# Pauses between the pieces of a norm in a three-stage kernel (attention, mixture of experts, gated layer): other numbers in three tables

## The chip, the cores and the metric

The kernel runs on one core of a Trainium2 chip. The metric is the time of one execution in device microseconds (us). The core's engines are TensorE (PE, matmuls; PEld is its weight load), VectorE (DVE), ScalarE (ACT), GpSimd (POOL) and SyncE (SP, which only issues transfers). Each engine runs its own instructions in the order in which the program wrote them, and waits for others through semaphores.

## The reference, cut to what matters

Attention over 8 heads of 576 positions for 4 batches gives 2304 tokens of 512 numbers. A mixture of 8 experts follows (all tokens through all experts, summed with the weights P). The last layer, in which the change lies, is this:

```python
rms = np.sqrt(np.mean(x * x, axis=-1, keepdims=True) + 1e-06)
xn = x / rms * rms_g
g = xn @ w_gate
silu = g * (1.0 / (1.0 + np.exp(-g)))
val = xn @ w_val
return (silu * val @ w_out).astype(np.float32)
```

Only the division by rms is told of below as "the norm" (rms_g is multiplied into the weights beforehand).

## The kernel before

**Tokens.** The 2304 tokens are three quads of 768 (`qd` 0, 1, 2: the first, second and third quad), each six blocks of 128. All matmuls take float32 operands as a high and a low part, and a product of two 2x2 block matrices is made of seven block products instead of eight. So an operand is kept as seven blocks (k = 0 to 6), each with its high and low part: three plain ones (k = 0 to 2) and four sums and differences (k = 3 to 6).

**Order of the program.** It is written by hand. The main loop counts ticks; whenever `bg.pump()` is called a tick passes, and queues of small steps (`Queue`) hand out those that have come due: an item runs when its lag, counted from the one before it, has passed. Where an item stands in the program is thus set by its lag in ticks; when it runs on the chip, by what its engine finds ahead of it and what it waits for.

**From the experts to the last layer.** The last expert's second half takes the third quad, then the second, then the first. As soon as a quad's sum `acc[:, qd]` is done (DVE, line 1907), four things happen to it:

1. Scaling (`norm_scale`, one run for blocks 0 to 2 and one for 3 to 5): ACT squares three blocks and sums the squares (L1504), DVE makes means (L1507), POOL takes the root (L1511), ACT multiplies three blocks (L1514). `evict_1` puts these steps into `scales[0]` or `scales[1]`.
2. Turning (`turn_tile`, `norm_turn`): PE transposes a block (L1521), ACT copies it back (L1523; in the third quad DVE does every other one, L1525). It first forces out what is left of the block's scaling.
3. Pieces (`norm_blocks`, queue `norm`): blocks i and 3 + i are one piece, so a quad has three. A piece has eight steps: `plain` (ACT L1538 makes high parts, DVE L1539 low parts), `add1` (DVE), `keep` (writes three plain blocks to DRAM, tensor xnd; two transfers, L1551), `add2` (DVE), three times `part` (ACT L1538, DVE L1539), `keep2` (writes the four other blocks; four transfers for the first and second quad, L1579). The first and second quad are written from POOL's queue. All pieces of a quad use the same two scratch areas, for which the accumulators of the next quad serve, so that a `plain` must wait until the `keep` before it has been read out, and a `part` for the `keep2` before it.
4. Loads (`load_block`, L1203, SP's queue): block k of the whole quad, 768 KB with both parts, is read back from xnd into one of nine slots. Plain blocks need the `keep` of all three pieces, the others the `keep2` of all three.

The lags of the pieces come from two tables, one entry per quad (first, second, third): `BLOCK_LAG` is the lag of each step and `BLOCK_GAP` what is added ahead of the second and third piece.

```python
steps = [plain, add1, keep], [add2, lambda: part(0, 1), lambda: part(1, 2), lambda: part(3, 1), keep2]
plain, more = [[(BLOCK_LAG[qd], f) for f in x] for x in steps]
gap = BLOCK_GAP[qd] if i else REST * (qd == 0)
return [(BLOCK_LAG[qd] + gap, steps[0][0])] + plain[1:], more
```

**The last layer** takes the third quad, then the second, then the first, each in two rounds; these six rounds are called 3a, 3b, 2a, 2b, 1a, 1b here (two more passes over all quads follow). A round has 14 steps. In each step PE makes one block product into one of two banks `ub` (L1271, six matmuls), from which ACT copies (L1439) or DVE adds (L1303); a bank is written again two steps later. The order of the blocks in a half round is k = 0, 1, 4, 3, 5, 2, 6. From round 3b on, two down products (L735 to L737, three matmuls each) of the round before stand behind most steps; in 3a transposes of the second quad (steps 3 to 8) and of the first (steps 9 to 14) stand there. "2a.3" below is step 3 of round 2a.

`Queue.add` appends steps whose first lag counts from the queue's last step (a queue idle for long hands out the first at the next tick); `Queue.follow` counts it from now. In the block that the change touches, `n == NGP - 2` is the second quad; the `else` branch serves the third (`NGP - 3`) and the first (`NGP - 1`).

Of the kernel before, what the change touches and what calls it, by code (L numbers as in the profile page):

```python
# [114 lines left out]
def kernel(  # L115
# [51 lines left out]
    LAG = 12  # L167
    FIRST_X = 8
    TURN_AT = (29, 30, 31, 32, 33, 34)
    BLOCK_LAG = (1.4, 1.0, 1.0)  # L170
    BLOCK_GAP = (6, 2, 0)
    LAST_TURN = {2 + i: (2, i) for i in range(6)} | {8 + i: (1, i) for i in range(6)}
    SCALE_LAG = 14
    REST = 10
    Y0_AT = (7, 10, 13, 16, 19)
    READ = 7
    LAST_READ = 16
# [1350 lines left out]
    def norm_blocks(qd, i, spare):  # L1528
# [42 lines left out]
        def part(k, n):  # L1571
            src = (b12, tab, tab, b21)[k]
            parts(src, high_of(k, n), src.bitcast(F32R))
            return 256 * n
# [9 lines left out]
# [6 lines that stand above are left out]
    with tc.manual_schedule():  # L1590
# [117 lines left out]
        for g in range(1, len(groups)):  # L1708
            due = SL * (first[g] // TA) - 4 * (LOOK + (PRE if groups[g][0] else 0)) - DUE
            steps = [step for t in ticks[last[g - 1] + 1 : last[g] + 1] for step in t]  # L1710
# [68 lines left out]
        for idx in range(-LOOK, n1 - LOOK):  # L1779
# [8 lines left out]
            if u.f == 0:  # L1788
                if "x" not in u.cell:
                    fetch(u)  # L1790
                if u.left:
                    bg.add(gate(u.t0, u.n, u.cell["x"]), 20)
                    if u.at:
                        area = fa[:, :1280], fa[:, 1280:3328].bitcast(F32R)
                        steps = sums(0, us[0].cell["x"], *area) if u.at == 1 else []
# [5 lines left out]
                else:  # L1801
# [5 lines left out]
                    steps = []  # L1807
# [20 lines left out]
            if not u.left and u.f == 0:  # L1828
                begin_psum()
                place = db[2], db[5], acc[:, 0, 0], wgc2  # L1830
                steps = []
# [26 lines left out]
        scales = [Queue(bg), Queue(bg)]  # L1858
        turns = {}

        def tile_of(qd, b):
            return 6 * qd + 2 * (b % 3) + b // 3
# [27 lines left out]
        def evict_1(n, k):  # L1890
            g, hh, qd = groups[n]
            half, col = OUT[k]
            a = acc[:, qd, 3 * half : 3 * half + 3]
            ps = threes[PAIR[k]].rearrange("p (m n) -> p m n", m=3)
            if col is None:
                a = a.rearrange("p m (c n) -> p m c n", c=2)
                ps = ps[:, :, None, :].to_broadcast([P, 3, 2, 256])
            else:
                a = a[:, :, 256 * col : 256 * (col + 1)]
            if (hh == 0 or g < E - 1) and k in (0, 2, 3, 4):  # L1900
                bg.drain(("expert", qd, half, col if half else None))
                nc.scalar.copy(a, ps)  # L1902
            elif (g, hh) == (E - 1, 1):
                if k in (0, 2, 3):
                    bg.drain(("expert", qd, half, col if half else None))
                for m in range(3):
                    nc.vector.scalar_tensor_tensor(
                        out=a[:, m], in0=ps[:, m], scalar=prob[:, tile_of(qd, 3 * half + m), g : g + 1],
                        in1=a[:, m], op0=ALU.mult, op1=ALU.add,
                    )  # L1910
                    bg.vector(512 if col is None else 256)
            else:
                nc.vector.tensor_tensor(out=a, in0=ps, in1=a, op=ALU.add)  # L1913
                bg.vector(1536 if col is None else 768)
            at = 2 * (g - E_STD) + hh + 1
            if n % NQD == NQD - 1:
                if n < NGP - 1:
                    product_2[at](k)
                elif k >= 3:
                    prepare_2(E, (0, 2, 1, 3)[k - 3], LAST_READ if k == 3 else STEP)  # L1920
            if (hh == 0 or g < E - 1) and k in (1, 5, 6):
                args = (g, hh, qd) + ((1, 0) if k == 1 else (0, None) if k == 5 else (1, 1))
                if early is None:
                    close_region(*args)
                else:
                    early.append(args)
            if (g, hh) == (E - 1, 1) and k >= 5:
                steps = norm_scale(qd, 3 * (k - 5))
                if n == NGP - 2:
                    scales[k - 5].follow([(SCALE_LAG, lambda: None)] + steps, ("scale", qd))  # L1930
                else:
                    short = 0.5 if n == NGP - 1 else 1
                    scales[k - 5].add([(short * lag, f) for lag, f in steps], ("scale", qd))

        early = []

# [105 lines left out]
        for n, (g, hh, qd) in enumerate(groups):  # L2042
# [12 lines left out]
            if n == 2:  # L2055
                waiting_for, early = early, None
                bg.add([lambda a=a: close_region(*a) for a in waiting_for], 12, bg.now + 8)
            if n in Y0_AT:
                i = 4 * Y0_AT.index(n)
                first_sums([divmod(x, 6) for x in range(i, min(i + 4, NTILE))])  # L2060
# [19 lines left out]
            for r in range(2):  # L2080
# [7 lines left out]
                for i, (wk, xk, which, begins) in enumerate(PROD):  # L2088
                    product((a, b)[which], w_block(region(g, j), wk), x_view(xmap[xk]), begins)
                    outcome_1(i, a, b, rd)  # L2090
                    if n < 2 and i in ((3, 6) if (n, r) == (0, 0) else (1, 6)):
# [4 lines left out]
                        steps = [lambda to=free_part: columns_2(totals, to)]  # L2096
# [100 lines left out]
        steps = 14  # L2197
        done = None
        nmap, nfree = xmap, free
        for n, (p, qd) in enumerate(passes):  # L2200
# [10 lines left out]
            for j in range(NG // 2):  # L2211
# [10 lines left out]
                if fresh and p:  # L2222
                    k = PROD[0][1]
                    load_block(nmap[k], True, qd2, k)
                for ci, s in enumerate((2 * j, 2 * j + 1)):
# [5 lines left out]
                    if fresh and p == 0 and ci == 1:  # L2231
                        k = PROD[0][1]
                        left.append((nmap[k], True, qd2, k))
                    for i, (wk, xk, which, begins) in enumerate(PROD):
# [23 lines left out]
                        if fresh and ci == 1 and i < 6:  # L2258
                            k = PROD[i + 1][1]
# [52 lines left out]
```

## Time and profile before

| | us |
|---|---|
| three runs | 2055.06, 2059.94, 2064.48 (median 2059.94) |
| profiled execution | 2053.64, of which its span (first to last instruction) is 2051.9 |
| PE busy | 2001.2 (98% of the span) |
| DVE, ACT, POOL busy | 1585.4, 1315.9, 296.4 |

The first two lines are times of whole executions; the profile's rows count from the first instruction of the profiled one. PE's matmuls are pipelined, so "busy" also holds stretches at a lower clock. The mean granted clock of PE is 0.991 of full speed.

### The profile page before, as it was taken

What the parts mean: (1) busy time and instruction counts of PE and PEld (TensorE: products, weight loads), DVE (VectorE), ACT (ScalarE), POOL (GpSimd) and SP (SyncE); (2) the same over time, 40 slices, a digit from 0 to 9 for tenths busy, and PEclk for the clock granted to TensorE, in tenths of its full rate; (3) what the DMA queues carried; (4) which work ended last, traced back from release to release, by engine and by line L of the source; (5) the groups of instructions that cost most, each with busy time, mean ns of one, the idle gap of its engine ahead of it and who ended that gap; (6) DMA issues with size and microseconds to landing.
All of it is one profiled execution on the core that took longest, in us unless ns stands there. A gap on an engine that the chain in (4) does not pass through costs nothing.

```text
span 2051.9 us, 37537 instructions
## 1 busy us (share of the span) xinstructions
PE 2001.2 (98%) x13611; PEld 1921.3 (94%) x13611; DVE 1585.4 (77%) x3364; ACT 1315.9 (64%) x2938; POOL 296.4 (14%) x340
## 2 busy tenths in 40 slices
PE   8999999999999999999999999999998988999999
PEld 7889888999999999999999999999998877888998
DVE  3677757889887888878787798888888657988645
ACT  6766335777777778878787777767766633423422
POOL 6443300001111111111011111111100220000000
PEclk9999999999999999999999999999999999999999
DMA  7688586577989889898888879778777775454341
GB/s 193 166 240 215 172 277 208 199 247 181 293 221 264 238 223 263 219 288 213 241 213 229 253 184 264 190 211 236 201 216 221 251 232 198 120 187 157 127 151 62
DMA packets 343577, 434.24 MB, mean 212 GB/s; under 512 B 81248, under 2 KB 242976, under 8 KB 343264
## 3 DMA queue, kind: packets, MB, share of 16 engines
q1 hardware_dynamic: 301360, 352.47, 52.8%
q0 software_dynamic: 42032, 79.38, 20.8%
q8 instruction: 107, 1.75, 0.3%
q14 instruction: 78, 0.64, 0.1%
HBM read 301.75 MB, written 130.02 MB: 210 GB/s over the span
## 4 chain that ended last, share of the span: by engine, by line
PE 83%; DVE 7%; DMA 4%; ACT 3%; issue 2%; POOL 1%; SPq 0%; POOLq 0%; DVEq 0%; ACTq 0%
PE ub L1271 36%; PE db L1881 28%; PE db L737 2%; PE db L736 2%; PE db L735 2%; DMA xt<-xdt 2%; PE psh L735 2%; PE psh L736 2%; PE psh L737 2%; PE psy L735 1%; PE ps_s L505 1%; PE psy L736 1%; PE psy L737 1%; PE ps_o L574 1%; DVE fa L1303 1%
## 5 line engine op out<-in xcount | busy, mean ns | idle before, releaser
L1271 PE MATMUL ub<-xt,w1t 128*128 128x384 f32 x2328 | 470.9, 339 | 12.2 <-DMA xt<-xnd 6.5
L1271 PEld LDWEIGHTS ub<-xt,w1t 128*128 128x128 f32 x2328 | 397.1, 190 | 18.2 <-issue 7.8
L1271 PE MATMUL ub<-xx,w1t 128*128 128x384 f32 x1956 | 394.5, 338 | 10.8 <-DMA xx<-xnd 7.6
L1881 PE MATMUL db<-w2t,ht 128*128 128x256 f32 x2772 | 380.9, 282 | 3.4 <-DVE ht L1299 1.9
L1881 PEld LDWEIGHTS db<-w2t,ht 128*128 128x128 f32 x2772 | 368.7, 189 | 3.9 <-DVE ht L1299 2.1
L1271 PEld LDWEIGHTS ub<-xx,w1t 128*128 128x128 f32 x1956 | 332.5, 190 | 17.0 <-issue 6.9
L1881 PE MATMUL db<-w2t,hx 128*128 128x256 f32 x2520 | 345.9, 282 | 2.2 <-DVE hx L1299 1.7
L1881 PEld LDWEIGHTS db<-w2t,hx 128*128 128x128 f32 x2520 | 333.9, 189 | 3.2 <-DVE hx L1299 1.9
L1303 DVE TENSOR_TENSOR fa<-ub,fa 128x384 f32<-128x384 f32 x360 | 199.2, 554 | 166.3 <-PE ub L1271 158.9
L1422 ACT ACTIVATE fa<-fa 128x384 f32<-128x384 f32 x252 | 132.4, 525 | 168.5 <-DVE fa L1303 168.1
L1950 POOL DMA_DIRECT2D y1d<-acc x99 | 113.9, 1150 | 798.3 <-DVE acc L1913 323.3
L1299 DVE TENSOR_TENSOR ht<-fa,ht 128x384 fp32r<-128x384 f32 x344 | 189.0, 551 | 22.2 <-ACT ht L1296 21.3
L1943 ACT ACTIVATE acc<-acc,prob 128x256 f32<-128x256 f32 (+1 forms) x351 | 190.7, 572 | 12.5 <-DVE acc L1913 12.2
L1296 ACT ACTIVATE ht<-fa 128x384 fp32r<-128x384 f32 x344 | 177.5, 518 | 27.4 <-DVE fa L1474 25.8
L1299 DVE TENSOR_TENSOR hx<-fa,hx 128x384 fp32r<-128x384 f32 x316 | 174.1, 551 | 26.1 <-ACT hx L1296 24.8
L1296 ACT ACTIVATE hx<-fa 128x384 fp32r<-128x384 f32 x316 | 162.4, 519 | 44.3 <-DVE fa L1474 40.9
L1377 DVE TENSOR_TENSOR fa<-fa 128x384 f32<-128x384 f32 x336 | 185.3, 551 | 5.2
L1414 ACT COPY fa<-ub 128x384 f32<-128x384 f32 x252 | 119.4, 474 | 93.1 <-PE ub L1271 92.3
L1913 DVE TENSOR_TENSOR acc<-db,acc 128x768 f32<-128x768 f32 (+1 forms) x117 | 142.9, 1221 | 39.0 <-PE db L1881 38.8
L1902 ACT COPY acc<-db 128x768 f32<-128x768 f32 x156 | 124.6, 799 | 14.5 <-PE db L1881 9.4
L1439 ACT COPY fa<-ub 128x384 f32<-128x384 f32 x108 | 51.6, 479 | 104.3 <-PE ub L1271 102.2
L1031 DVE TENSOR_TENSOR w1t<-fa,w1t 128x256 fp32r<-128x256 f32 (+1 forms) x160 | 83.4, 524 | 19.1 <-ACT w1t L1028 19.1
(269 smaller groups left out, 3091.9 us busy)
## 6 DMA issues: line engine op xcount, KB each, us to landing
xt<-xdt SPq DMA_DIRECT2D x111, 768.0 KB
xx<-xdt SPq DMA_DIRECT2D x92, 768.0 KB
y1d<-acc POOLq DMA_DIRECT2D x72, 384.0 KB, 8.4
y1d<-acc POOLq DMA_DIRECT2D x36, 768.0 KB, 8.6
xt<-xnd SPq DMA_DIRECT2D x25, 768.0 KB
xx<-xnd SPq DMA_DIRECT2D x24, 768.0 KB
fa<-in_moe_w_dram SPq DMA_DIRECT2D x56, 256.0 KB
raw<-in_moe_w_dram SPq DMA_DIRECT2D x52, 256.0 KB
```

The costliest lines, as they stand in the source:

```text
L1271: nc.tensor.matmul(ps[:, :TH], w[i][:, c], x[:, k, c], start=first and c == 0 and n == 0, stop=c == 1 and n == 2, skip_group_check=True,)
L1296: nc.scalar.activation(h[0], src, func)
L1299: engine.tensor_tensor(out=h[1], in0=src, in1=h[0].bitcast(F32), op=ALU.subtract)
L1303: nc.vector.tensor_tensor(out=out, in0=ps, in1=more, op=ALU.add)
L1377: nc.vector.tensor_tensor(**kw)
L1414: nc.scalar.copy(z[nm], ps)
L1422: nc.scalar.activation(z[nm], z[nm], AF.Relu)
L1881: nc.tensor.matmul(spot(k, m), hm[x], w[y], start=BEGIN[k] and r == 0 and m != 1 and i == 0, stop=r == 1 and i == 2, skip_group_check=True,)
L1902: nc.scalar.copy(a, ps)
L1913: nc.vector.tensor_tensor(out=a, in0=ps, in1=a, op=ALU.add)
L1943: nc.scalar.activation(a, a, AF.Copy, scale=prob[:, tile_of(qd, b), g : g + 1])
L1950: nc.gpsimd.dma_start(out=y, in_=t, accum_op=ALU.add)
```

## The change

Four numbers change, and one is new. The second quad's steps have a lag of 0.8 ticks instead of 1.0, and nothing is added ahead of its second and third piece (2 before). The first quad gets 2 added ticks instead of 6 there. The scaling of the third and of the first quad begins with an empty step of 3 ticks counted from now (`follow`) instead of at once (`add`); within it the first quad keeps its half lags. No instruction is added or taken away; PE's and POOL's instructions stand in the same order as before.

```diff
-    BLOCK_LAG = (1.4, 1.0, 1.0)
-    BLOCK_GAP = (6, 2, 0)
+    BLOCK_LAG = (1.4, 0.8, 1.0)
+    BLOCK_GAP = (2, 0, 0)
...
     SCALE_LAG = 14
     REST = 10
+    AFTER = 3
...
                 else:
                     short = 0.5 if n == NGP - 1 else 1
-                    scales[k - 5].add([(short * lag, f) for lag, f in steps], ("scale", qd))
+                    scales[k - 5].follow([(AFTER, lambda: None)] + [(short * lag, f) for lag, f in steps], ("scale", qd))
```

The new line moves all later lines by one: what is L1504 before is L1505 in the changed kernel.

On ACT, at the beginning of round 3a, these rows stand between the last expert and the layer's first copies. L1514 with `acc` is the multiplication of the scaling, L1504 the square; the first six multiplications belong to the second quad, all other scaling here to the first. L1439 is the copy that empties bank `ub`, L1523 the copy of a turned block. Before:

```order
L1514 ACTIVATE acc<-acc,cv 128x512 x5
L1504 ACTIVATE cv<-acc 128x512 x2
L1514 ACTIVATE acc<-acc,cv 128x512
L1504 ACTIVATE cv<-acc 128x512
L1514 ACTIVATE acc<-acc,cv 128x512 x3
L1504 ACTIVATE cv<-acc 128x512 x2
L1439 COPY fa<-ub_4251 128x384
L1504 ACTIVATE cv<-acc 128x512
L1457 ACTIVATE fa<-fa 128x384
```

In the changed kernel the same place reads:

```order
L1515 ACTIVATE acc<-acc,cv 128x512 x6
L1505 ACTIVATE cv<-acc 128x512 x3
L1440 COPY fa<-ub_4251 128x384
L1458 ACTIVATE fa<-fa 128x384
L1440 COPY fa<-ub_4251 128x384
L1515 ACTIVATE acc<-acc,cv 128x512 x2
L1505 ACTIVATE cv<-acc 128x512
```

Three multiplications and two squares of the first quad moved from ahead of the round's first L1439 to behind it; a third square, which stood right behind it, moved further back too.

On ACT in round 3b, L1538 makes the high parts of the second quad's pieces, L1457 is the sigmoid and L1439 the copy out of `ub`. Before, these rows stand there, from the second piece's `plain` (the first two L1538) to the first row of the third piece's `plain` (the last row, behind the copy of step 3b.8):

```order
L1538 ACTIVATE acc<-acc 128x512
L1538 ACTIVATE acc<-acc 128x256
L1439 COPY fa<-ub_4251 128x384
L1439 COPY fa<-ub_4252 128x384
L1538 ACTIVATE acc<-acc 128x256
L1457 ACTIVATE fa<-fa 128x384
L1538 ACTIVATE acc<-acc 128x512
L1457 ACTIVATE fa<-fa 128x384
L1538 ACTIVATE acc<-acc 128x256
L1457 ACTIVATE fa<-ub_4251 128x384
L1439 COPY fa<-ub_4252 128x384
L1538 ACTIVATE acc<-acc 128x512
```

In the changed kernel, from the second piece's three `part` steps (the first three rows):

```order
L1539 ACTIVATE acc<-acc 128x256
L1539 ACTIVATE acc<-acc 128x512
L1539 ACTIVATE acc<-acc 128x256
L1440 COPY fa<-ub_4251 128x384
L1440 COPY fa<-ub_4252 128x384
L1539 ACTIVATE acc<-acc 128x512
L1539 ACTIVATE acc<-acc 128x256
L1458 ACTIVATE fa<-fa 128x384
L1539 ACTIVATE acc<-acc 128x256
L1458 ACTIVATE fa<-fa 128x384
L1539 ACTIVATE acc<-cv 128x512
```

The two L1439 in the middle are those of steps 3b.3 and 3b.4 in both. Before, the second piece's parts stand behind them, spread between three sigmoids; in the changed kernel the parts stand ahead of them and the third piece's `plain` right behind.

On SP, ahead of round 1a, L1203 loads the first quad's seven blocks; L840 and L882 fetch and store other weights. Before:

```order
L840 DMA cv<-in_moe_w_out_dram 128x512
L882 DMA m2o<-cv 128x256
L1203 DMA xx<-xnd 128x2x768 x2
L840 DMA fa<-in_moe_w_out_dram 128x512
L882 DMA m2o<-cv 128x256
L1203 DMA xt<-xnd 128x2x768 x4
L1203 DMA xx<-xnd 128x2x768
```

In the changed kernel:

```order
L1204 DMA xx<-xnd 128x2x768
L841 DMA cv<-in_moe_w_out_dram 128x512
L883 DMA m2o<-cv 128x256
L1204 DMA xx<-xnd 128x2x768
L1204 DMA xt<-xnd 128x2x768 x2
L841 DMA fa<-in_moe_w_out_dram 128x512
L1204 DMA xt<-xnd 128x2x768
L883 DMA m2o<-cv 128x256
L1204 DMA xt<-xnd 128x2x768
```

The first load moved ahead of a fetch and a store, and the third to fifth ahead of the second store; the last two (one more xt, and an xx behind the last row) still stand behind it.

## Rows read from the trace of the kernel before

**Rows 1.** Page: busy us and share of the span by engine.
```profile
PE 2001.2 (98%) x13611; PEld 1921.3 (94%) x13611; DVE 1585.4 (77%) x3364; ACT 1315.9 (64%) x2938; POOL 296.4 (14%) x340
```

**Rows 2.** Waits of PE from 1500 to 1800: total, times, longest us.
```profile
PE ub L1271 <- DMA xx<-xnd: 7.6, 2, 6.5
PE ub L1271 <- DMA xt<-xnd: 5.8, 1, 5.8
```

**Rows 3.** Timeline of PE: start, us, what; in brackets idle before it.
```profile
1539.70 0.60 PE L1521 MATMUL db<-ident,acc 128*128 128x128 f32 x4
...
1592.70 2.25 PE L1271 MATMUL ub<-xt,w1t 128*128 128x384 f32 x12
1599.13 2.24 PE L1271 MATMUL ub<-xt,w1t 128*128 128x384 f32 x6 [4.18 <-ACT fa L1439]
...
1618.54 0.59 PE L1271 MATMUL ub<-xt,last_r 128*128 128x384 f32 x2
...
1649.65 2.26 PE L1271 MATMUL ub<-xx,w1t 128*128 128x384 f32 x6 [6.46 <-DMA xx<-xnd]
...
1699.38 1.29 PE L1271 MATMUL ub<-xx,w1t 128*128 128x384 f32 x6 [1.15 <-DMA xx<-xnd]
1701.38 2.05 PE L1271 MATMUL ub<-xx,w1t 128*128 128x384 f32 x6 [0.71 <-DVE cv L854]
...
1711.43 4.10 PE L1271 MATMUL ub<-xt,w1t 128*128 128x384 f32 x12 [5.83 <-DMA xt<-xnd]
```

**Rows 4.** Stretches: length, busy us (count) by engine, PE's granted clock, DMA.
```profile
1540.00:1560.00 20.00, 18.28 (x133) 17.88 (x132) 16.68 (x38) 11.48 (x24) 0.00 (x0) 1.00 0.50 143
1572.00:1580.00 8.00, 5.84 (x36) 5.64 (x36) 7.50 (x18) 4.96 (x12) 0.00 (x0) 0.79 0.85 237
1599.10:1603.40 4.30, 4.27 (x17) 4.14 (x18) 1.28 (x3) 2.70 (x6) 0.85 (x1) 0.60 1.06 407
1600.00:1616.00 16.00, 16.00 (x101) 15.62 (x100) 9.78 (x19) 13.34 (x29) 2.61 (x3) 0.92 0.84 315
1649.60:1653.60 4.00, 3.95 (x12) 3.83 (x13) 0.00 (x0) 0.48 (x1) 0.00 (x0) 0.50 1.01 398
1701.40:1705.60 4.20, 4.20 (x12) 3.39 (x12) 3.29 (x9) 0.74 (x2) 0.00 (x0) 0.59 1.03 395
1711.40:1715.40 4.00, 3.97 (x13) 3.83 (x14) 0.00 (x0) 0.48 (x1) 0.00 (x0) 0.52 1.03 411
```

**Rows 5.** Chain that ended last: start, us, what.
```profile
1635.93 5.12 DMA xnd<-acc
...
1641.16 8.35 DMA xx<-xnd
```

**Rows 6.** The same chain 60 us later.
```profile
1699.33 7.66 DMA xnd<-acc
...
1707.00 4.29 DMA xt<-xnd
```

**Rows 7.** Timeline of POOL: second quad, second `keep2` and third `keep`.
```profile
1632.01 3.07 POOL L1579 DMA_DIRECT2D xnd<-acc  x4 [5.74 <-ACT acc L1538]
1635.07 1.69 POOL L1551 DMA_DIRECT2D xnd<-acc  x2
```

**Rows 8.** Timeline of ACT.
```profile
1540.92 0.53 ACT L1422 ACTIVATE fa<-fa 128x384 f32<-128x384 f32 x1 [1.15 <-DVE fa L1303]
...
1591.53 0.63 ACT L1504 ACTIVATE cv<-acc 128x512 f32<-128x512 f32 x1 [1.05 <-DVE acc L1907]
...
1595.40 1.94 ACT L1514 ACTIVATE acc<-acc,cv 128x512 f32<-128x512 f32 x3 [1.16 <-POOL cv L1511]
1598.62 0.46 ACT L1439 COPY fa<-ub 128x384 f32<-128x384 f32 x1
...
1625.53 0.48 ACT L1439 COPY fa<-ub 128x384 f32<-128x384 f32 x1 [0.56 <-PE ub L1271]
...
1632.85 0.94 ACT L1538 ACTIVATE acc<-acc 128x512 fp32r<-128x512 f32 x2
```

## The prediction

> **What bounds the kernel now.** I began with the page: PE is busy 98% of the span [rows 1], so only stretches in which PE stops can give much. Four numbers for the norm can move only the passage from the experts to the last layer, so I looked at PE's waits there, then at the timeline around each. PE waits twice for blocks in `xx` and once for one in `xt`, 7.6 and 5.8 us, all read back from xnd [rows 2]. The reader is to see three stops:
>
> - Stop A, 3a.3: PE waits 4.18 us for ACT's copy of the bank that 3a.1 filled [rows 3].
> - Stop B, 2a.1: 6.46 us for a load [rows 3]. The chain of waits goes back from that load (8.35 us) to the third `keep` (its write took 5.12 us) [rows 5]. POOL issued this `keep` right behind the second piece's `keep2`, with no pause between the two [rows 7].
> - Stop C, 1a.1 to 1a.3: 1.15, 0.71 and 5.83 us, 7.7 in all [rows 3]. The last comes from a write of `keep2` (7.66 us) and the load behind it (4.29 us) [rows 6].
>
> Each stop costs more than its length, since the granted clock is down afterwards: 0.50 behind B, 0.59 and 0.52 around C, 0.60 behind A [rows 4], between full speed and half, as stretches mix 2.4 and 1.2 GHz. Busy time times (1 - clock) is what that costs: 3.95 x 0.50 = 2.0 us at B, 4.20 x 0.41 + 3.97 x 0.48 = 3.6 at C, 4.27 x 0.40 = 1.7 at A. So A costs 5.9, B 8.5 and C 11.3 us. No more than these 25.7 us can be had.
>
> **Part 1: the first quad's scaling, later (stop A).** Before, ACT reached the copy for A at 1598.62, though PE had filled the bank by about 1594 (twelve matmuls of two products from 1592.70, 2.25 us) [rows 3, 8]. Ahead of the copy stood the first quad's scaling, among it three multiplications that had waited 1.16 us for POOL's root and took 1.94 us [rows 8]. In the changed order only three squares stand there. The first begins when it did, at 1591.53, and its sums wait for DVE as before [rows 8]; at 0.63 us and a short read-out each, three end at about 1593.7. The copy then takes 0.46 and is done by 1594.5, before PE ends its second product at 1594.95. Stop A goes: +5.9 us.
>
> The work isn't gone; it now stands inside 3a. In 16 us of that round ACT was busy 13.34 us [rows 4], so 2.7 us were free. Into it go three multiplications (1.94), two squares (0.63 and a read-out, some 0.7 each) and, since the pieces come earlier, some 1.3 us of high parts (a `plain`, 0.94, and one `part` of under half of that) [rows 8]: 4.6 us, 2 more than fit. PE can be only two steps ahead of the copies. Following ACT's changed order row by row, I find PE short of a copied bank by 0.5 us near 3a.7, 0.3 at 3a.9 and 2.0 at 3a.10, where five rows of the norm stand ahead of the copy: -2.8 us. Is the clock lost there too? Waits of 1.15 and 0.71 us within 2 us were followed by a clock of 0.59 [rows 3, 4], so I count 1.7 us for these as well. Part 1 gives 5.9 - 2.8 - 1.7 = +1.4 us. Bounds: 0 (all of it comes back as waits for ACT) and 5.9.
>
> **Part 2: the third quad's scaling, later.** `follow` starts it three ticks later, but the turning forces out what is left, so its first block is multiplied just ahead of the transposes. In the changed ACT order the three multiplications stand behind the L1422 that ran at 1540.92, which had waited 1.15 us for DVE; the first transposes ran at 1539.70 [rows 3, 8]. With ACT and DVE a little freer before, I get the first block at 1541.2, a wait of 1.5 us. Half of it is made good, since PE waits for DVE's copy after the next two groups anyway: -0.7 us. Bounds: 0 and -2.3 (L1422 where it was, one multiplication of 0.65 behind it, nothing made good). The waits of under a microsecond between 1540 and 1560 left the clock at 1.00 [rows 4], so no clock is counted here.
>
> **Part 3: the second quad's pieces (stop B).** The third piece's `plain` ran at 1632.85; in the new order it stands right behind the copy of 3b.4, which ran at 1625.53 [rows 8]: 6.9 us earlier against PE. With PE itself ahead by 1.4 (part 1) that is about 1624.5. Now what was slack becomes a wait: this `plain` writes where the second piece's `keep` is still being read out. By the changed order that `keep` is issued near 1619.5, and read out some 5 us later, by the 5.12 of the row [rows 5], so `plain` runs near 1625. The third `keep` then queues on POOL behind the second `keep2` (3.07 us): issued near 1626.5 instead of 1635.07 [rows 7], written 5.9 us later (5.12 from its second transfer on) at 1632.4. Its load, taken at 8.35 us again [rows 5] because writes are still under way, ends near 1640.8. PE came to 2a.1 at 1643.2 (1649.65 - 6.46) [rows 3], and comes at 1641.8 with part 1. The load is in time by 1 us.
>
> Two things come late in its place. DVE makes the low parts of that `plain` only when the `keep` before it is read out, and the sums of 3b.5 and 3b.6 (L1303) stand behind it: PE waits about 1.0 us at 3b.7 and 0.6 at 3b.8. And the third `keep2` is written at about 1640, after which the four sum blocks follow each other at the pace of the queue (4.29 us for one alone [rows 6], near 2 each in a row); 2a.4 and 2a.6 may wait 0.7 us. Part 3 gives 8.5 - 1.6 - 0.7 = +6.2. Bounds: 8.5, and 2 (as much as part 1 brings PE forward, the pieces held wholly by the reuse of their areas).
>
> **Part 4: the first quad's pieces (stop C).** Its pieces begin some six steps earlier, as they follow the second quad's, and the last `keep2` stands at 2b.4 instead of 2b.13: nine steps of (1643.2 - 1618.54) / 14 = 1.76 us [rows 3], 15.9 us. Stop C is 7.7 us of waiting. The loads then go out when the blocks of 2b free their slots. On SP the third to fifth come ahead of a store that they stood behind; the last two remain behind it, and they are needed only at 1a.6 and 1a.7. So C goes in full: +11.3. Bounds: 6, if the clock is lost to other waits in the same place or the last loads come late, and 11.3. What hides the norm in 2a and 2b is DVE and ACT with free time, but a denser norm may hold a copy: -0.7 (0 to -2).
>
> **The sum.** 1.4 - 0.7 + 6.2 + 11.3 - 0.7 = 17.5 us. The profiled execution took 2053.64 (its span 2051.9 and 1.7 around it), so it becomes 2036.1. It is 6.3 below the median of the three runs; taken from the median of 2059.94 the sum gives 2042.4, which I round to 2042 as what runs of the changed kernel should show. The bounds add to 5.7 us (0 - 2.3 + 2 + 6; the last -2 is part of C's 6) and 25.7 us.
>
> **Rivals.** Changes under 0.5% (10.3 us) can't be told from none here.
>
> (a) *Short waits that keep the clock down.* Each of the new waits (3b.7 and 3b.8 together, 2a.4, 2b) is followed by half-speed matmuls. For: 0.79 granted from 1572 to 1580, when PE was busy 5.84 of 8 us [rows 4]. Against: the clock of 1.00 from 1540 to 1560. At 1.7 us for each of two to three, 5 us go: 2047. The Trainium skill, "TensorE: Matmul & The Clock Gate", section on HAM oscillation, says that waits for transfers between groups of matmuls throttle PE again, so that each group starts cold; by that rule the number of waits counts and this case holds. The trace bears it out only for waits of near 2 us and more, as the two stretches show.
>
> (b) *The pieces stand earlier but don't run earlier.* Each `part` waits for the `keep2` before it to be read out, so a quad's three pieces keep a period of their own: the last two `keep2` writes issued 7 us apart already, POOL hardly idle between them [rows 7]. Then B keeps most of its 8.5, the first quad follows late, and C loses its lower bound's 5 us. 1.4 - 0.7 + 2 + 6 - 0.7 = 8 us: 2052, not to be told from no change. Against it: the second piece's `keep2` had waited 5.74 us for ACT [rows 7], which is pause, not period.
>
> (c) *Slower.* In 3b ACT and DVE wait for writes inside their queues, PE stops at every few steps, and the clock stays at its lower level. A product of six matmuls took 2.26 us at B, as long as two at full speed (2.25) [rows 3], so at worst a round of 24.7 us takes twice as long. One round takes the whole gain; a round and a half costs 37 us: 2079. It decides when waits of 2 us come as often as from 1572 to 1580 (2.2 us idle in 8 [rows 4]), all through 3b and half of 2a. Against it: in 3a, where ACT is fuller than in 3b, the clock was 0.92 even with stop A's end in it [rows 4].
>
> **How the numbers follow.** The forecast as worked out, all three stops nearly gone, 0.52 (2035 to 2046); (a) 0.22 at 2047; (b) 0.17 at 2052; (c) 0.05; the rest, 0.04, is more than forecast (A's full 5.9 kept). The range of 2031 to 2054 leaves out (c), the end of (b) and the runs that lie lower than 25.7 us of gain. Faster by over 0.5% (below 2049.6): the forecast, most of (a), the rest: 0.78. Within 0.5%: (b) and a little of (a): 0.17. Slower: 0.05.
>
> **What would show it.** Right: no wait of PE for a load from xnd above 1.5 us at 2a.1 and 1a.1 to 1a.3; granted clock near 1.00 after them; the wait for L1439 at 3a.3 gone, and one of about 2 us for L1440 near 3a.10 in its place; POOL's third `keep` of the second quad some 8 us earlier; a wait of 1 to 1.5 us ahead of the first transposes of the third quad. Wrong: 2a.1 still waits more than 3 us, with ACT or DVE waiting for a write ahead of a piece (then b), or a clock under 0.8 over all of 3b without one long wait (then c). The forecast is most open in part 1: if ACT's backlog in 3a is absorbed, 4.5 us more come.

## The result, and the profile after

| | before | changed | ratio, 95% interval |
|---|---|---|---|
| median, first comparison | 2057.53 us (4 runs) | 2041.12 us (4 runs) | 0.9916 [0.9889, 0.9943] |
| median, second comparison (E5 below) | 2055.32 us (11 runs) | 2041.21 us (6 runs) | 0.9931 [0.9913, 0.9949] |
| profiled execution | 2053.64 us | 2041.57 us | |
| its span, mean clock of PE | 2051.9 us, 0.991 | 2039.6 us, 0.995 | |

The change made the kernel faster by 0.7 to 0.8%, near the forecast of 2042. By medians it gained 16.4 and 14.1 us, with intervals of 12 to 23 and of 10 to 18. From one profiled execution to the other it gained 12.1 us, where the sum said 17.5. So some terms are wrong, and the trace says which.

PE's busy time hardly moved. From the page of the changed kernel (answers to [rows 1]):

```profile
PE 1998.0 (98%) x13611; PEld 1918.3 (94%) x13611; DVE 1586.4 (78%) x3364; ACT 1316.0 (65%) x2938; POOL 296.9 (15%) x340
```

PE's waits from 1500 to 1800 in the changed kernel (answers to [rows 2]; total, times, longest):

```profile
PE db L1522 <- ACT acc L1524: 2.0, 1, 2.0
PE db L738 <- DVE ht L1300: 2.0, 1, 2.0
...
PE ub L1272 <- DMA xt<-xnd: 0.8, 1, 0.8
PE ub L1272 <- DMA xx<-xnd: 0.8, 2, 0.5
```

The loads from xnd, 13.4 us of waiting before, now cost 1.6. New are waits for ACT and DVE, the two of 2.0 us above all. Where do they stand? PE runs the same instructions in the same order in every kernel here, so the start of one row in both traces gives PE's lead over the kernel before at that place, and the change of the lead between two places says what the stretch between them gave. First six marks in the trace of before, beside 1592.70 and 1618.54 of [rows 3] (timeline of PE):

```profile
1538.64 1.23 PE L1881 MATMUL db<-w2t,hx 128*128 128x256 f32 x9
...
1603.35 0.60 PE L1521 MATMUL db<-ident,acc 128*128 128x128 f32 x4
...
1640.24 0.51 PE L1271 MATMUL ub<-xx,w2t 128*128 128x384 f32 x2
...
1653.97 0.40 PE L736 MATMUL db<-w2t,hx 128*128 128x512 f32 x1
...
1697.37 0.39 PE L735 MATMUL db<-w2t,ht 128*128 128x512 f32 x1
...
1716.76 2.25 PE L1271 MATMUL ub<-xt,w1t 128*128 128x384 f32 x12
```

The same eight rows in the changed kernel, with the waits between them (timeline of PE; answers to [rows 3]):

```profile
1539.76 1.23 PE L1882 MATMUL db<-w2t,hx 128*128 128x256 f32 x9
1542.21 0.66 PE L1522 MATMUL db<-ident,acc 128*128 128x128 f32 x4 [1.22 <-ACT acc L1515]
...
1594.42 3.29 PE L1272 MATMUL ub<-xt,w1t 128*128 128x384 f32 x18
...
1599.06 0.60 PE L1522 MATMUL db<-ident,acc 128*128 128x128 f32 x4
...
1605.83 0.65 PE L1522 MATMUL db<-ident,acc 128*128 128x128 f32 x4 [2.01 <-ACT acc L1524]
...
1608.61 1.31 PE L1272 MATMUL ub<-xt,w1t 128*128 128x384 f32 x6 [0.65 <-DVE fa L1461]
...
1611.43 1.33 PE L1272 MATMUL ub<-xt,w1t 128*128 128x384 f32 x6 [1.07 <-ACT fa L1440]
...
1618.92 0.59 PE L1272 MATMUL ub<-xt,last_r 128*128 128x384 f32 x2
...
1623.71 0.50 PE L738 MATMUL db<-w2t,ht 128*128 128x512 f32 x1 [2.00 <-DVE ht L1300]
...
1637.70 2.38 PE L1272 MATMUL ub<-xt,w2t 128*128 128x384 f32 x12 [1.04 <-DVE fa L1461]
...
1644.78 0.51 PE L1272 MATMUL ub<-xx,w2t 128*128 128x384 f32 x2
...
1647.56 1.24 PE L1272 MATMUL ub<-xx,w1t 128*128 128x384 f32 x6
...
1650.70 0.40 PE L737 MATMUL db<-w2t,hx 128*128 128x512 f32 x1
...
1697.97 0.39 PE L736 MATMUL db<-w2t,ht 128*128 128x512 f32 x1
...
1698.67 2.26 PE L1272 MATMUL ub<-xx,w1t 128*128 128x384 f32 x12
...
1705.64 2.25 PE L1272 MATMUL ub<-xt,w1t 128*128 128x384 f32 x12
```

The lead is 1538.64 - 1539.76 = -1.12 us before the norm even begins (it arose in the stages ahead, so it isn't of the change), and 1716.76 - 1705.64 = +11.12 at the end. The stops A (3a.3), B (2a.1, at 1647.56) and C (1a.1 to 1a.3, from 1698.67) have no wait left. Their gain is partly given back between them.

The table holds this balance for all runs: what PE's lead over the kernel before gained (+) or lost (-) between the marks, in us. The columns end at the rows that stand at 1592.70 (3a.1), 1603.35, 1618.54 (3b.1), 1640.24, 1653.97, 1697.37 and 1716.76 before. The first column holds part 2 (0.45 us) and a jitter of -1.1 to +0.8 that comes and goes.

| run | to 3a.1 | stop A | rest of 3a | 3b | stop B | 2a, 2b | stop C | sum |
|---|---|---|---|---|---|---|---|---|
| forecast | -0.7 | +5.9 | -4.5 | -1.6 | +8.5 | -1.4 | +11.3 | +17.5 |
| changed | -0.60 | +6.01 | -4.67 | -4.16 | +7.81 | -3.87 | +11.72 | +12.24 |
| E1 scaling only | +0.30 | +6.01 | -5.44 | -0.20 | +0.82 | -0.58 | -0.38 | +0.53 |
| E2 tables only | -0.23 | +0.01 | -0.17 | -2.62 | +7.80 | -4.42 | +11.72 | +12.09 |
| E3 second quad only | -0.30 | 0.00 | -0.17 | -4.15 | +7.79 | -3.48 | +10.93 | +10.62 |
| E4 first quad only | +0.75 | -0.63 | -0.49 | -0.01 | +1.53 | -4.02 | +11.64 | +8.77 |
| E5 changed, again | +0.32 | +6.01 | -6.04 | -4.13 | +7.78 | -3.91 | +11.73 | +11.76 |
| E6 DVE turns | -1.57 | +6.01 | -4.30 | -2.58 | +7.56 | -4.85 | +11.73 | +12.00 |
| E7 lag 0.7 | +0.33 | +6.01 | -6.06 | -3.48 | +8.54 | -4.61 | +11.73 | +12.46 |
| E8 scaling spread | -0.71 | +6.01 | -5.63 | -4.15 | +7.80 | -3.84 | +11.73 | +11.21 |
| E9 weights later | +0.32 | +6.04 | -2.65 | -4.38 | +7.80 | -4.38 | +11.73 | +14.48 |
| E10 first quad rests | -0.60 | +6.01 | -4.83 | -4.15 | +8.62 | -3.94 | +11.73 | +12.84 |
| E11 lag 0.7, weights | -0.60 | +6.03 | -2.65 | -3.33 | +8.54 | -4.42 | +11.72 | +15.29 |
| E12 combined | +0.75 | +6.01 | -2.62 | -3.71 | +7.28 | -4.25 | +11.73 | +15.19 |

The two executions of the changed kernel (changed, E5) agree within 0.1 us in most columns, but differ by 0.9 ahead of 3a.1 and by 1.4 in the rest of 3a. The runs of one kernel scatter by several microseconds. So the medians say whether a kernel is faster, and the balance says where.

### The profile page after: what moved, and what is told of

The parts are those of the page before. It is cut to its first block, busy times and chain, and to the rows that moved or that the text cites. A ratio compares the mean times of both kernels' runs of the same rounds, so it can differ in the third digit from the quotient of the medians.

```text
span 2039.6 us, 37535 instructions
## 1 busy us (share of the span) xinstructions
PE 1998.0 (98%) x13611; PEld 1918.3 (94%) x13611; DVE 1586.4 (78%) x3364; ACT 1316.0 (65%) x2938; POOL 296.9 (15%) x340
## 4 chain that ended last, share of the span: by engine, by line
PE 84%; DVE 6%; DMA 4%; ACT 2%; issue 2%; POOL 0%; SPq 0%; DVEq 0%; POOLq 0%; ACTq 0%
PE ub L1272 37%; PE db L1882 28%; PE db L738 2%; PE db L737 2%; PE db L736 2%; DMA xt<-xdt 2%; PE psh L736 2%; PE psh L737 2%; PE psh L738 2%; PE psy L736 1%; PE ps_s L506 1%; PE psy L737 1%; PE psy L738 1%; PE ps_o L575 1%; DVE fa L1304 1%
## 5 line engine op out<-in xcount | busy, mean ns | idle before, releaser
L1304 DVE TENSOR_TENSOR fa<-ub,fa 128x384 f32<-128x384 f32 x360 | 199.7, 555 | 158.2 <-PE ub L1272 152.0
L1300 DVE TENSOR_TENSOR ht<-fa,ht 128x384 fp32r<-128x384 f32 x344 | 189.4, 552 | 20.7 <-ACT ht L1297 19.7
L1300 DVE TENSOR_TENSOR hx<-fa,hx 128x384 fp32r<-128x384 f32 x316 | 174.5, 552 | 27.9 <-ACT hx L1297 26.9
```

The source lines that it names most:

```text
L1300: engine.tensor_tensor(out=h[1], in0=src, in1=h[0].bitcast(F32), op=ALU.subtract)
L1304: nc.vector.tensor_tensor(out=out, in0=ps, in1=more, op=ALU.add)
```

## The experiments

Each has runs of the kernel before on the same chip beside it.

**E1 to E4: which edit does what.** E1 has the tables of before, E2 the scaling of before, E3 and E4 one quad's part of the tables.

```diff
# E1: the scaling of the change, the tables of before
+    AFTER = 3
...
-                    scales[k - 5].add([(short * lag, f) for lag, f in steps], ("scale", qd))
+                    scales[k - 5].follow([(AFTER, lambda: None)] + [(short * lag, f) for lag, f in steps], ("scale", qd))
# E2: the tables of the change (E3: GAP 6, 0, 0), the scaling of before
-    BLOCK_LAG = (1.4, 1.0, 1.0)
-    BLOCK_GAP = (6, 2, 0)
+    BLOCK_LAG = (1.4, 0.8, 1.0)
+    BLOCK_GAP = (2, 0, 0)
# E4: LAG and scaling of before
-    BLOCK_GAP = (6, 2, 0)
+    BLOCK_GAP = (2, 2, 0)
```

> The scaling of the third and first quad begins three ticks later, as in the changed kernel; the tables of the pieces are those of before. Theory S (the waits of 3a come from the scaling): stop A goes, 6.0 us; the three waits of the second half of 3a that the changed kernel showed (2.01, 0.65 and 1.07 us for ACT and DVE) stand here too and take 4.5 back; the first transposes wait 1.2 us, 0.5 after what is made good. Round 3b begins 1.0 us earlier, stops B and C stay, and B's load follows PE only in part: 0 to 1.5 us faster than before, 2053 against a median of 2054 to 2058. Theory P (those waits come from the pieces that stand earlier): no wait above 0.5 us in the second half of 3a, 5.5 us kept up to 3b.1; with B and C growing only in part, 2.5 to 5.5 us faster.

> The tables of the pieces as in the changed kernel; the scaling begins at once, as before. Stop A stays: 4.2 us and the clock behind it. Theory S: no waits in the second half of 3a, but those of 3b (2.00 for DVE at the first down products with a clock of 0.62 behind it, 1.04 at 3b.8) stay, as they come from the second piece's plain and sums ahead of the DVE row that PE needs; B and C gone. Sum: -4.3 in 3b, +7.8 at B, -3.9 in 2a, +12.0 at C, so 11.6 us faster than before, the same as the changed kernel within 1.5 us, ratio 0.9944. Theory P: the waits of 3a come too, 3.7 to 4.5 us less: 7 us faster, ratio 0.9965.

> Only the second quad's two numbers (lag 0.8, nothing added); first quad's pause of 6 ticks and the scaling as before. The last keep2 of the first quad then stands at 2b.8, between 2b.13 of before and 2b.4 of the changed kernel. Theory R (either half of the table is enough for stop C, since its loads can go out only from 2b.7 on when slots come free): the write and the load of 12 us (7.66 + 4.29) from 2b.8 end seven steps later at about 1a.1, so C shrinks from 7.7 us of waiting to 0 to 3: B +7.8, 3b -4.3, 2a -2 to -4, C +8 to +12: 10 to 13 us faster. Theory H (each half of the table gives its share of C): C keeps 4 us of waiting and its clock, 4 to 7 us faster.

> Only the first quad's pause, 2 ticks instead of 6; the second quad's pieces and the scaling as before. Its last keep2 stands at 2b.9. Stops A and B stay, round 3b has no new wait. Theory R (either half of the table is enough for C): keep2 is written and loaded by about 1a.2, one step ahead of the first sum block, C keeps 0 to 3 us of waiting and loses little clock: 8 to 12 us faster than before. Theory H: C keeps half, 4 to 6 us faster. If the waits of 2a (0.78, 0.54, 0.52 and 1.05 us, 3.9 us in all in the changed kernel) come from the first quad's denser pieces they show here as well, 1 to 3 us.

| | median us | ratio to before, 95% interval |
|---|---|---|
| E1 | 2055.64 | 0.9997 [0.9987, 1.0007] |
| E2 | 2042.65 | 0.9944 [0.9929, 0.9958] |
| E3 | 2042.86 | 0.9937 [0.9923, 0.9952] |
| E4 | 2046.03 | 0.9955 [0.9941, 0.9969] |

The later scaling alone is worth nothing that the runs can tell, and the tables alone can't be told from the whole change (12.09 us by the balance, 12.24 and 11.76 with the scaling). E1 shows theory S: stop A goes (+6.01), and the rest of 3a takes 5.44 back, without any earlier piece; E2, which keeps stop A, has no loss there. Theory P falls. E1's timeline of PE shows the new wait in 3a:

```profile
1607.45 0.66 PE L1522 MATMUL db<-ident,acc 128*128 128x128 f32 x4 [3.04 <-ACT acc L1524]
```

E3 and E4 show theory R: either half of the table takes stop C away (+10.93 and +11.64 of 11.72). The two halves aren't independent: 10.62 + 8.77 = 19.4 against E2's 12.09. Each of them alone still leaves one of the first quad's loads late: PE waits 0.98 and 1.01 us for it at 1a.6, and 1.9 and 1.7 us are lost from 1716.76 to 1800 (0.1 in E2). The loss in 3b comes with the second quad's numbers alone (E4: -0.01), the one in 2a and 2b with either.

**E5 to E8: what holds 3a and 3b.** E5 is the changed kernel once more. E6 lets DVE copy the second quad's turned blocks, E7 lowers the lag once more, E8 spreads the scaling.

```diff
# E6, in norm_turn
-        if qd < NQD - 1 or t % 2:
+        if qd == 0 or qd == 2 and t % 2:
# E7
-    BLOCK_LAG = (1.4, 0.8, 1.0)
+    BLOCK_LAG = (1.4, 0.7, 1.0)
# E8
-                    short = 0.5 if n == NGP - 1 else 1
+                    short = 1 if n == NGP - 1 else 1
```

> The changed kernel once more, as a yardstick for the next ones on the same chip. By the first four runs the tables of the pieces bring all of the gain and the scaling none: a ratio of 0.992 to 0.9945 to the kernel before, the same as the tables alone (0.9944) within what the intervals tell apart. If the scaling did bring its predicted 1.4 us or more beside the tables, it lies at 0.9925 or below.

> The changed kernel, and in 3a the six turned blocks of the second quad are copied back by DVE instead of ACT. Theory S (ACT's total work is the limit in the second half of 3a: 4.00 of 4 us busy in three windows): six copies of 0.57 us, about 3 us, leave ACT, and DVE, busy 1.1 to 1.8 of 4 us up to 1608, has room; the waits of 2.01, 0.65 and 1.07 us shrink to 1 us or less, and the lost 4.65 us of 3a to 1: 3 to 4.5 us faster than the changed kernel. Theory O (the order on the queues is the limit, since DVE's mean waits for ACT's squares and everything behind it on DVE waits too): the same waits appear with DVE's copies as their cause, and the time is that of the changed kernel within 1 us.

> The changed kernel with a lag of 0.7 instead of 0.8 for the second quad: its second piece's plain stands at 3a.13 instead of 3a.14, the third at 3b.2 instead of 3b.4. Theory B (the pieces have reached the period that the reuse of their areas sets): the third keep is issued no more than 1 us earlier against PE, DVE rows wait longer behind pieces, the loss in 3b grows from 4.15 us to 5 to 7: 1 to 3 us slower than the changed kernel. Theory W (the wait of 2.00 us at the first down products of 3b comes only from where the second piece's plain and sums stand): they now stand ahead of the rows of 3b.1, the wait goes and with it the clock of 0.62 behind it: 2 to 3.5 us faster.

> The changed kernel with the first quad's scaling at whole lags instead of half ones, so that it is spread over 3a.1 to 3a.12 instead of 3a.1 to 3a.8. Theory S1 (the scaling makes a heap on ACT in the middle of 3a): fewer rows stand ahead of the copies of 3a.7 to 3a.10, the three waits fall from 3.73 us to 1 or 2: 2 to 3 us faster than the changed kernel. Theory S2 (it is ACT's total that counts, and what is spread meets the pieces and the first quad's turning at 3a.9 to 3a.14): the waits move back to the second half of the round in the same sum, and transposes wait for a block not yet scaled: the same time within 1 us.

| | median us | ratio to before, 95% interval |
|---|---|---|
| E5 | 2041.21 | 0.9931 [0.9913, 0.9949] |
| E6 | 2039.92 | 0.9920 [0.9903, 0.9937] |
| E7 | 2040.41 | 0.9925 [0.9907, 0.9943] |
| E8 | 2040.89 | 0.9928 [0.9908, 0.9949] |

None can be told from E5. E5 can't be told from E2 (0.9944) either, so no gain of the scaling beside the tables is shown. E6 takes work off ACT and E8 spreads it, and 3a loses as before them (-4.30 and -5.63): ACT's work alone isn't the limit there. What else is, stands in ACT's timeline. Before, the high part of the weights `w2t` (L1138, L1139 in the others) began without a wait; in the changed kernel and in E5 ACT stood still ahead of it (a fence each, in this order):

```profile
1603.92 0.64 ACT L1138 ACTIVATE w2t<-w2t 128x512 fp32r<-128x512 f32 x1
```

```profile
1602.69 0.63 ACT L1139 ACTIVATE w2t<-w2t 128x512 fp32r<-128x512 f32 x1 [1.74 <-DMA w2t<-m2o]
```

```profile
1601.52 0.63 ACT L1139 ACTIVATE w2t<-w2t 128x512 fp32r<-128x512 f32 x1 [3.09 <-DMA w2t<-m2o]
```

The chain that ended last, in the changed kernel (start, us, what), goes through this transfer, and so does PE's wait of 2.01 us for L1524 at 1605.83:

```profile
1590.38 12.29 DMA w2t<-m2o
1602.69 0.63 ACT w2t L1139
...
1605.30 0.47 ACT acc L1524
```

SP issued the transfer behind the loads from xnd, and the queue was full: between 1585 and 1605 the DMA view of the changed kernel lists these, with the size of each, and the engines' share was 103%:

```profile
q1 hardware_dynamic: 3168, 7.73, 103.2%
...
xt<-xnd SPq DMA_DIRECT2D x3, 768.0 KB
xx<-xnd SPq DMA_DIRECT2D x3, 768.0 KB
...
w2t<-m2o SPq DMA_DIRECT2D x4, 256.0 KB
```

That the full queue makes it slow is likely, but no run emptied the queue. It was as full before (103.1%). In the seven traces in which ACT waits for this transfer, ACT could begin 12.2 to 12.4 us after its issue. Before, it was issued at 1588.28, so by an estimate from these it landed at about 1600.6, and ACT, held up by the scaling ahead of stop A, came at 1603.92. Stop A had been the cover of these weights.

The balance says how much of 3a's loss this is. Where ACT waits for `w2t`, 1.74 to 3.09 us, the loss less this wait is 2.35 to 3.09 us (changed 2.93, E5 2.95, E1 2.65, E6 2.35, E7 3.09, E8 2.68, E10 2.94). In E5 ACT waits 1.35 us longer than in the changed kernel, and 3a loses 1.37 more. So the wait passes to PE nearly in full, and a part of about 2.6 us remains that isn't the transfer.

In E6 the stall only changes its name: DVE's low part (L1142) waits for ACT's high part, then DVE's mean (L1508) 1.29 us for ACT's squares, and PE for the DVE row behind both (E6, timeline of ACT, of DVE and of PE):

```profile
1604.18 0.63 ACT L1139 ACTIVATE w2t<-w2t 128x512 fp32r<-128x512 f32 x1 [1.95 <-DMA w2t<-m2o]
```

```profile
1604.84 0.69 DVE L1142 TENSOR_TENSOR w2t<-w2t 128x512 fp32r<-128x512 f32 x1 [1.70 <-ACT w2t L1139]
...
1607.50 0.55 DVE L1304 TENSOR_TENSOR fa<-ub,fa 128x384 f32<-128x384 f32 x1
```

```profile
1608.11 1.32 PE L1272 MATMUL ub<-xt,w1t 128*128 128x384 f32 x6 [2.21 <-DVE fa L1304]
```

So theory O was right about E6's time and about DVE's wait for the squares, though the first cause is the transfer, which neither theory had named.

E7 answers for the pieces. POOL's third `keep` of the second quad, in the changed kernel, in E5 and in E7 (timeline of POOL, a fence each; the last row of [rows 7] is that of before):

```profile
1630.19 1.69 POOL L1552 DMA_DIRECT2D xnd<-acc  x2 [0.93 <-ACT acc L1539]
```

```profile
1629.04 1.68 POOL L1552 DMA_DIRECT2D xnd<-acc  x2 [0.94 <-ACT acc L1539]
```

```profile
1627.53 1.69 POOL L1552 DMA_DIRECT2D xnd<-acc  x2
```

Against 3b.1 (1618.92, 1617.77 and 1616.25) it is issued 11.27, 11.27 and 11.28 us later; before it was 1635.07 - 1618.54 = 16.53. The change brought it 5.3 us forward; the next step of the lag brings nothing. This is theory B's mark. In the changed kernel neither ACT nor DVE waits for a write to xnd between 1600 and 1650; in E7 ACT does, ahead of the third piece's first `part` (timeline of ACT):

```profile
1628.58 0.42 ACT L1539 ACTIVATE acc<-acc 128x256 fp32r<-128x256 f32 x1 [2.84 <-DMA xnd<-acc]
```

Theory B's price isn't paid: the wait of 2.00 at 3b.2 shrinks to 0.57, waits of 0.92 (3b.2), 1.36 (3b.7) and 0.54 (3b.8) come for it, and 3b loses 3.48 instead of 4.13.

**E9 to E12: the weights' high parts later, the first quad later, both and more.**

```diff
# E9, E11, E12: the wait ahead of the last layer's first high part
-    LAST_READ = 16
+    LAST_READ = 20
# E10 (E12: 13)
-    REST = 10
+    REST = 16
# E11, E12
+    BLOCK_LAG = (1.4, 0.7, 1.0)
# E12 also: the third quad's scaling by add
```

> The changed kernel; the four high parts of the last layer's weights w2t that ACT makes in 3a are due four ticks later (20 instead of 16), nothing else. Theory D (with stop A gone ACT reaches the first of them before its transfer has landed, and waits 1.74 to 3.09 us for it with the copies of 3a behind it, as every run with the later scaling showed): the wait for w2t goes, PE's wait for L1524 with it, the loss in 3a falls from 4.65 to 5.9 us to 1 to 2, and 3 to 4.5 us more of stop A are kept: 2 to 4.5 us faster than the changed kernel. Theory S (ACT's total work in the second half of 3a): ACT's work is the same, the waits of 3a only take other places, same time within 1 us.

> The changed kernel; the first quad's first piece starts six ticks later (a rest of 16 instead of 10), at 2a.2 instead of 3b.12, its last keep2 stands at 2b.7 instead of 2b.4. Theory T (round 2a loses 3.9 us because the first quad's first writes and pieces fall between the second quad's loads): PE's waits for xt and xx in 2a (0.73, 0.64 and 0.50 us) go or halve and those for DVE move: 1 to 3 us faster than the changed kernel, if stop C stays gone. Theory K (those loads wait for the second quad's own last keep2 and then follow each other at the pace of the queue): the loads land as before, the waits stay, and with keep2 at 2b.7 stop C takes 0 to 2.7 us back (2b.8 gave 2.7): same, or up to 3 us slower.

> The changed kernel with both edits: lag 0.7 for the second quad and the weights' high parts four ticks later. If the two gains are independent (3b kept about 1.2 us more with 0.7, the weights 2 to 4.5 us): 3 to 6 us faster than the changed kernel, a ratio to the kernel before of 0.990 to 0.992. If PE's earlier arrival only waits again (at 2a.1 to 2a.6 for the second quad's loads, which start by the writes and not by PE): half of it, 1 to 3 us.

> The changed kernel with four edits: lag 0.7 for the second quad, the weights' high parts four ticks later, the third quad's scaling at once again, and a rest of 13 for the first quad. By the pieces measured so far: 1.2 us in 3b, 2 to 3 us in 3a, 0.5 us at the third quad's first transposes, 0 to 1.5 us in 2a: 4 to 6 us faster than the changed kernel, a ratio to the kernel before of 0.989 to 0.991, if they add. If PE, coming earlier, waits for the second quad's loads in 2a instead, a ratio of 0.991 to 0.992, as the two edits alone gave (0.9915). The wait at the first transposes shows part 2 by itself: 1.22 us with the later scaling, gone here.

| | median us | ratio to before, 95% interval |
|---|---|---|
| E9 | 2038.12 | 0.9912 [0.9898, 0.9926] |
| E10 | 2041.18 | 0.9926 [0.9911, 0.9941] |
| E11 | 2038.69 | 0.9915 [0.9902, 0.9928] |
| E12 | 2040.80 | 0.9931 [0.9915, 0.9948] |

E9 settles 3a. ACT doesn't wait for `w2t` any more, PE's wait for L1524 is gone, and 2.65 us are lost instead of 4.67 and 6.04 (timeline of ACT, then of PE):

```profile
1607.67 0.67 ACT L1139 ACTIVATE w2t<-w2t 128x512 fp32r<-128x512 f32 x1
```

```profile
1605.55 1.31 PE L1272 MATMUL ub<-xt,w1t 128*128 128x384 f32 x6 [0.53 <-DVE fa L1461]
...
1607.86 1.31 PE L1272 MATMUL ub<-xt,w1t 128*128 128x384 f32 x6 [0.56 <-ACT fa L1440]
```

So theory D holds: 2.0 and 3.4 us less are lost than in the two executions of the changed kernel, whose waits for `w2t` were 1.74 and 3.09. E9 doesn't by itself refute theory S, since it also moves work: two of the four high parts, some 0.6 us each, now stand in 3b (at 1617.98 and 1622.97, behind 3b.1 at 1616.17), where all four stood in 3a. E6, which takes more than that off ACT and keeps the wait, does. By the balance E9 is 2.2 to 2.7 us better than the changed kernel, and E11 3.0 to 3.5 (15.29 against 12.24 and 11.76); by medians their ratios are lower than E5's but the intervals overlap, so a better kernel is likely, not shown. E12's balance is that of E11, while its runs (2036.50 to 2044.25) don't show it. It does show part 2: with the third quad's scaling at once the wait of 1.22 us ahead of the first transposes is gone.

E10 refutes theory T in its aim: 2a's waits for loads shrink (0.16 and 0.72 us are left, against theory K), but DVE is late in 2b instead, and 2a and 2b lose the same 3.94 (timeline of PE):

```profile
1688.57 2.38 PE L1272 MATMUL ub<-xt,w2t 128*128 128x384 f32 x12 [1.89 <-DVE fa L1461]
```

Stop C stays away, as its row in the table says, so theory K's price isn't paid.

## Why the prediction was right, and where its steps were not

**The time** came out as forecast by luck: two errors cancel. The gain was put at 17.5 us; the medians differ by 14.1 to 16.4, the profiled executions by 12.1, the passage itself by 12.2. And the base, the median of three runs (2059.94), was high: four later series of before have medians of 2055.86, 2055.32, 2055.12 and 2055.75 (17, 11, 11 and 11 runs). The mechanism, three stops that go and a part of them that comes back as shorter waits, is what the trace shows, but the largest of the shorter waits have other causes than those forecast.

**Part 1** gave 6.01 - 4.67 = +1.3 us in the changed kernel, 0.0 in E5 and 0.6 in E1, against +1.4 forecast. The step "following ACT's changed order row by row" failed: it took each row as ready when ACT came to it. One of them, the weights' high part, hangs on a transfer for which ACT stood until some 12.3 us after its issue, in every trace in which it waited. Without that wait the term of 2.8 us comes out in size (E9 loses 2.65 in 3a), but not in place: PE waits 0.53 us at 3a.9 and 0.56 at 3a.10, where 0.5 at 3a.7, 0.3 at 3a.9 and 2.0 at 3a.10 were forecast. The 1.7 us of clock didn't come there in the changed kernel (1.00 in the first row below). That the transfer took back as much, 1.74 us, is luck: in E5 it took 3.09 (stretches of the changed kernel, answers to [rows 4]; the granted clock stands behind the brackets of POOL). Behind the places of B and C, in the last two rows, it is 1.00, where 0.50 to 0.59 stood before:

```profile
1600.00:1616.00 16.00, 12.27 (x80) 11.14 (x78) 9.11 (x19) 14.23 (x34) 2.63 (x3) 1.00 0.93 358
1623.70:1627.70 4.00, 3.99 (x14) 3.81 (x15) 3.39 (x8) 2.22 (x5) 1.51 (x2) 0.66 0.60 171
1647.50:1651.50 4.00, 3.47 (x18) 2.96 (x18) 3.81 (x9) 1.42 (x3) 0.67 (x1) 1.00 1.01 336
1698.60:1702.60 4.00, 4.00 (x23) 3.69 (x22) 3.93 (x11) 1.77 (x4) 0.00 (x0) 1.00 1.01 385
```

**Part 2**: -0.45 to -0.48 in every run with the later scaling of the third quad, -0.01 to -0.03 without; -0.7 was forecast.

**Part 3**: B gave 7.8 (8.5 forecast), though the third `keep` came 5.3 us earlier against 3b.1 and not "some 8". Its load was in time because PE was late: issued at 1635.72 and taken at 8.35 us [rows 5], it ends near 1644.1 by this estimate, and PE reached 2a.1 at 1647.56; without the 4.16 us lost in 3b PE would have come at 1643.4, and waited 0.7 us.

The term of 1.6 us for DVE in 3b was mis-sized: it is 4.16. A wait of 1.04 us stands at 3b.9, near the forecast one in size, but for another row (L1461), and no write holds a piece there; the forecast pair, for L1304 at 3b.7 and 3b.8, stands in E7 (1.36 and 0.54). What was missed is the wait of 2.00 at the down products of 3b.2. The second piece's `plain` moved to 3a.14, and on DVE its low parts (L1540) and the sums of `add1` (L1558, L1559) now stand ahead of the row that PE needs (L1300). DVE timeline of the changed kernel:

```profile
1621.36 1.03 DVE L1540 TENSOR_TENSOR acc<-acc 128x512 fp32r<-128x512 f32 x2 [0.51 <-ACT acc L1539]
1622.31 0.42 DVE L1558 TENSOR_TENSOR acc<-acc 128x256 f32<-128x256 f32 x1
...
1623.10 0.55 DVE L1300 TENSOR_TENSOR ht<-fa,ht 128x384 fp32r<-128x384 f32 x1
```

The forecast followed only the third piece, which it took for the one that decides; and behind this wait the clock fell to 0.66, for 4.16 - 2.62 = 1.5 us more (E2 has the same wait and no fall).

**Part 4**: C gave 11.72 (11.3 forecast). The two terms for 2a and 2b together were mis-sized: 0.7 for late loads and 0.7 for a held copy were forecast, 3.87 measured, in which the listed waits are 1.53 for loads (2a.5 to 2a.7) and 1.57 for DVE (2a.9 and 2b.2). E3, E4, E10 and E12, with four other places of the pieces, lose 3.5 to 4.3 as well; what exactly sets that sum stays open.

**The rivals.** (a) holds in part: in the changed kernel the clock fell once from 3a on, after the wait of 2.00 us at 3b.2, for 1.5 us (1.7 were named), and not after those of about 1 us. The Trainium skill, "TensorE: Matmul & The Clock Gate", section on HAM oscillation, tells of waits for transfers, longer than those of (a), after each of which a group starts cold. The rows bear this out for the three stops of before (0.50 to 0.60 behind 4.18 to 6.46 us) and, beyond the page, for some waits of 2 us, which were for other engines; from 3a on the changed kernel's waits of 1.1 us or less all left the clock at 1.00. (b) falls for the changed kernel: the pieces did run earlier; only at the lag of 0.7 (E7) does a piece wait for a write (2.84 us). The 7 us that (b) names lie between the `keep2` at 1632.01 and the last one, at 1639.16 in POOL's timeline of before, which [rows 7] doesn't show. (c) falls: the clock was below 1.00 in two of the stretches of 4 us from 1620 to 1640 (0.62 and 0.95).

## What to carry to other kernels

Before a stall is removed, look up what else used its time: here a transfer was ready in time because stop A and the work ahead of it brought ACT there late. With the stop gone, 1.7 to 3.1 of its 6.0 us came back as ACT's wait for the transfer, and some 2.6 were lost in 3a besides. When a trace shows a new wait, follow it to the first wait that is for a transfer, since moving or spreading the work in between (E6, E8) only renames it. Where steps of a queue are pulled forward, go through the rows of each engine that they pass, all pieces and not only the last, since each one costs PE what it puts ahead of the row that PE needs.

## What the runs showed of the hardware

The clock's answer to one and the same wait differed. The wait of 2.00 us at 3b.2, with PE idle for just as long, was followed by a granted clock of 0.66 in the changed kernel, 0.57 in E5 and in E3, and by 1.00 in E2 and E6. In 3a the wait at 3a.7, two shorter ones behind it, left it at 1.00 in the changed kernel (2.01 us), but in E5, the same kernel, at 0.64 (3.15 us); the wait of 3.16 us at 2a.9 of E12 left it at 1.00 (4 us from the wait's end on; E5 in 3a and in 3b, then E6):

```profile
1604.70:1608.70 4.00, 4.00 (x18) 3.62 (x19) 2.61 (x6) 4.00 (x10) 0.83 (x2) 0.64 1.06 420
1622.60:1626.60 4.00, 4.00 (x13) 3.67 (x14) 3.34 (x8) 2.00 (x5) 1.56 (x2) 0.57 0.61 175
```

```profile
1625.10:1629.10 4.00, 4.00 (x20) 3.68 (x21) 3.38 (x8) 2.90 (x7) 1.52 (x2) 1.00 0.60 171
```

So whether a wait near 2 us costs 2 or 3.5 us can't be read from its length.

A fall of the clock need not cost anything either. From the end of the wait at 3a.7 to 3b.1, PE took 13.11 us in E5, with the clock at 0.64 at first, and 13.09 in the changed kernel at 1.00: ACT was busy 4.00 of the next 4 us in both, and PE's later waits for ACT and DVE shrank from 1.72 to 0.26 us.

The listed idle isn't always the whole loss. In 3a the changed kernel's three waits sum to 3.73 us, and PE lost 4.67 there at a clock of 1.00; in 3b of E2, with its waits of 2.00, 0.16 and 1.06 us, 2.72 more than before, it lost 2.62.
